# Retention and a gated FFN on one core: the first two pairs of chunks interleaved, their weights in narrower tiles

## The chip, the core and the metric

The kernel runs on one core of a Trainium2 chip. Its engines work side by side, each through its own list of instructions in order: TensorE multiplies matrices (PE in the profile, with PEld for its weight loads), VectorE (DVE) and ScalarE (ACT) read what TensorE left in the PSUM banks and write it to the on-chip memory, GpSimd (POOL) prepares data in that memory, and SyncE (SP) issues the transfers. The metric is the device time of one execution in microseconds, the median of several; lower is better.

## What is computed

```python
scores = (1/8) * q @ k.T                       # 8 batches, 8 heads, 576 positions, 64 dimensions
ret    = scores * gamma[h] ** (i - j)          # for j <= i, else 0
x      = (ret @ v)                             # heads side by side: 4608 rows of 512
out    = (sigmoid(x @ w_gate) * (x @ w_val)) @ w_out     # 512 -> 1536 -> 512
```

The retention is computed in chunks of 128 positions. Within a chunk the masked product of q and k is multiplied with v ("intra"); what comes from earlier chunks is q times a running 64 by 64 state per head, the sum of k times v ("inter"). The powers of gamma are put on q and k when these are cast to bf16.

## The kernel before, in words

x is kept transposed on the chip (`xT`, 512 by 4608) and filled by chunks; the FFN runs over blocks of its columns. The first 768 columns are three *pairs* of chunks (`PAIRS`): pair 0 is positions 0 to 255 of batch 0, pair 1 is positions 256 to 511 of it, pair 2 is the first 256 of batch 1. The rest are 30 *steps* of 128 columns, each loaded, cast, turned by a DMA transposition (`cross`, L294, the tile T) and worked off in a slot between the matmuls of the FFN (`slot`, L543). The schedule is written by hand: each engine gets its instructions in the order in which the program issues them, and waits for semaphores of the others.

The change lies in the start, up to the first FFN block (columns 0 to 511, made from pairs 0 and 1). Its parts, by their functions:

- `load_pair` (L130) and `load_w` (L142) issue transfers of 256 KB on SP. The order now: k and q of both pairs, then v of both, then the first gate and value weights for 256 columns (`load_w(0, 2)`, four tiles of 128 by 2 by 256), then the next 256 columns, then the rest. Each transfer waits until the one eight places before it has landed; the load tiles are 18.
- `cast_pair` makes bf16 of k (with its powers, on POOL, L272), of q (with its powers, on DVE, L272) and of v (POOL, L269); `cast_w` makes bf16 of weights (L246). On POOL: k of both pairs, v of both, the first weights.
- `turn` transposes k or q of two heads pairs on TensorE (`pair_t`, L312) and copies the result with ACT (L322) to kT or qT. It needs a PSUM bank: TR and PV have one buffer each, QK two, the FFN's three, the state's one.
- `pair_qk` multiplies kT and qT (L331, 16 matmuls) and masks the result on DVE (L336, two instructions) to ptp.
- `first_st` adds k times v of one chunk to the state's bank (L362, 8 matmuls), `tile_sv` copies the state to `sbd` on ACT (L371, two instructions).
- `pair_intra` (L429, 8 matmuls) and `pair_inter` (L439, 4 matmuls) make a chunk's x in a bank, `pair_out` (L448) moves it to xT.
- `h_half` (L892) makes 256 columns of one gate or value of the FFN from four matmuls, `gate` (L898) is the sigmoid on ACT, and L895 the product of both on DVE. `h_both` (L816) then goes on with 512 columns at a time, from the third of the 12 pieces of 128 features on.
- `fill` (L183) is matmuls of a blank tile into an unused bank: no part of the result. Before the change there are 40 short ones at the start and four calls with 3, 2, 3 and 2 long ones.

The order now, from the last `fill`: pair 0 and pair 1 are turned and multiplied first (k and q alone), then come the states and values of pair 0, then those of pair 1 with the first two gates of columns 0 to 255 between them, then the remaining halves of the first two features pieces, and `h_both((2, 3))`.

Of the kernel before, what the change touches and what calls it, by code (L numbers as in the profile page):

```python
# [16 lines left out]
def kernel(  # L17
# [19 lines left out]
    nc = tc.nc  # L37
# [87 lines left out]
    def load_pair(A):  # L125

        b, a2 = PAIRS[A]
        for nm, src, g in (("k", k, 0), ("q", q, 0), ("k", k, 1), ("q", q, 1), ("v", v, 0), ("v", v, 1)):
            t = ld_pool.tile([P, M, 2, D], FP32, tag="ld", name=f"{nm}32p_{A}_{g}")
            nc.sync.dma_start(  # L130
                out=t.rearrange("p h r d -> p h (r d)"),
                in_=src[b, g * M:(g + 1) * M, a2 * 2 * P:(a2 + 1) * 2 * P, :].rearrange("h (p r) d -> p h (r d)", r=2))
            parts[nm, "pair", A, g] = t
            yield

    def load_w(f, nf):

        for nm, src in (("g", moe_w_gate), ("v", moe_w_val)):
            for i in range(nf):
                r = NKC // nf  # L140
                t = ld_pool.tile([P, r, nf * P], FP32, tag="ld", name=f"w{nm}32_{f}_{i}")
                nc.sync.dma_start(  # L142
                    out=t, in_=src[i * r * P:(i + 1) * r * P, f * P:(f + nf) * P].rearrange("(c p) f -> p c f", p=P))
                parts[nm, f, i] = t
# [3 lines left out]
        nc.sync.dma_start(out=t, in_=moe_w_out[f * P:(f + 1) * P, :])  # L148
        parts["o", f] = t

    both = [load_pair(A) for A in range(2)]
    for n_pair in (4, 2):
        for one in both:
            for _ in range(n_pair):
                next(one)
    load_w(0, 2)
    load_w(2, 2)
    load_w(4, 4)
    load_w(8, 4)
# [19 lines left out]
    def fill(n, parts=1):  # L179

        for i in range(n * parts):
            k = 4 // parts
            nc.tensor.matmul(idle[-1][:, 0:k, :], lhsT=blank, rhs=blank.unsqueeze(1).to_broadcast([P, k, P]),  # L183
                             start=True, stop=True)
# [58 lines left out]
    def cast_w(nm, f, nf, i, eng):  # L243
        r = NKC // nf
        at = (slice(None), slice(i * r, (i + 1) * r), slice(f * P, (f + nf) * P))
        eng(out=(wg_sb if nm == "g" else wv_sb)[at], in_=parts.pop((nm, f, i)))  # L246
# [12 lines left out]
    def cast_pair(nm, A, g, eng):  # L259

        if (nm, A) not in natural:
            natural[nm, A] = osb_pool.tile([P, 2, H, D], BF16, tag="osb", name=f"{nm}p_{A}")
        if nm != "v" and A == 2:
            o = natural[nm, A].rearrange("p r (m y) d -> p y m r d", y=2)[:, g]
        else:
            o = natural[nm, A][:, :, g * M:(g + 1) * M, :].rearrange("p r h d -> p h r d")
        i = parts.pop((nm, "pair", A, g))
        if nm == "v":
            eng(out=o, in_=i)  # L269
        else:  # L270
            tab = (ktab2 if nm == "k" else qtab2)[:, PAIRS[A][1], g * M:(g + 1) * M, :].unsqueeze(3).to_broadcast([P, M, 2, D])
            eng.tensor_tensor(out=o, in0=i, in1=tab, op=ALU.mult)  # L272
# [51 lines left out]
    def pair_qk(A, g, banks):  # L324
        ps = [psum.tile([P, 2, 2, P], FP32, tag=tag, name=f"qkp_{A}_{g}_{hh}") for hh, (psum, tag) in enumerate(banks)]
        for i in range(2):
            m = 2 * g + i
            for r in range(2):
                for a in range(2):
                    for hh in range(2):  # L330
                        nc.tensor.matmul(ps[hh][half(a), i, r, :], lhsT=turned["kp", A][half(hh), m, r, half(a)],  # L331
                                         rhs=turned["qp", A][half(hh), m, a * P:(a + 1) * P], start=True, stop=True)
        if g == 0:
            probs["p", A] = [att_pool.tile([P, M, 2, P], BF16, tag="T", name=f"ptp_{A}_{hh}", bufs=6) for hh in range(2)]
        for hh in range(2):
            nc.vector.tensor_tensor(out=probs["p", A][hh][:, 2 * g:2 * g + 2], in0=ps[hh],  # L336
                                    in1=trip.unsqueeze(1).to_broadcast([P, 2, 2, P]), op=ALU.mult)
# [18 lines left out]
    def first_st(A, a):  # L356

        if 0 not in st_tiles:
            st_tiles[0] = st_psum.tile([P, M, P], FP32, tag="st", name="st_0")
        for r in range(2):  # L360
            for m in range(M):
                nc.tensor.matmul(st_tiles[0][:, m, :], lhsT=natural["k", A][half(a), r, 2 * m:2 * m + 2, :],  # L362
                                 rhs=natural["v", A][half(a), r, 2 * m:2 * m + 2, :],
                                 start=(A == 0 and a == 0 and r == 0 and m == 0),
                                 stop=(A == 1 and a == 1 and r == 1 and m == M - 1), skip_group_check=True)

    def tile_sv(A, a, engs):
        b, a2 = PAIRS[A]
        sb = sbd[2 * A + a]
        for hh in range(2):  # L370
            engs[hh](out=sb[half(hh), :, half(hh)], in_=st_tiles[b][half(hh), :, half(hh)])  # L371
        state[b, 2 * a2 + a, 1] = sb
# [47 lines left out]
    def pair_intra(A, g, a):  # L420
        s = 2 * A + a
        if s not in pair_ps:
            pair_tile(A, a, [(tr_psum, "tr") if a else (pv_psum, "pv")])
        for i in range(2):
            m = 2 * g + i
            ps, at_m, of = pair_ps[s][m]
            for r in range(2):
                for hh in range(2):
                    nc.tensor.matmul(ps[half(hh), at_m, :], lhsT=natural["v", A][half(a), r, 2 * m + hh, :],  # L429
                                     rhs=probs["p", A][hh][half(a), m, r, :],  # L430
                                     start=(at_m == 0 and r == 0), stop=(at_m == of - 1 and r == 1),
                                     skip_group_check=True)
# [372 lines left out]
    def turn(nm, A, g, pool=ffn_psum, tag="ffn"):  # L805
        pair_t(nm, A, g, pool, tag, on_act)
# [23 lines left out]
    for A in range(2):  # L830
        for g in range(2):
            cast_pair("k", A, g, nc.gpsimd)
    for A in range(2):
        for g in range(2):
            cast_pair("v", A, g, on_pool)
    for i in range(2):
        cast_w("g", 0, 2, i, on_pool)
    for i in range(2):
        cast_w("v", 0, 2, i, on_pool)
    QK = [(qk_psum, "qk"), (qk_psum, "qk")]  # L840
    FF = [(ffn_psum, "ffn"), (ffn_psum, "ffn")]
    TR, PV = (tr_psum, "tr"), (pv_psum, "pv")
    cast_pair("q", 0, 0, nc.vector)
    turn("k", 0, 0, *TR)
    turn("q", 0, 0, *PV)
    fill(3)
    cast_pair("q", 0, 1, nc.vector)
    pair_qk(0, 0, QK)
    turn("k", 0, 1, *TR)
    fill(2)  # L850
    turn("q", 0, 1, *PV)
    fill(3)
    cast_pair("q", 1, 0, nc.vector)
    pair_qk(0, 1, FF)
    cast_pair("q", 1, 1, nc.vector)
    turn("k", 1, 0, *TR)
    turn("q", 1, 0, *PV)
    fill(2)
    turn("k", 1, 1, *TR)
    pair_qk(1, 0, QK)  # L860
    turn("q", 1, 1, *TR)
    first_st(0, 0)
    tile_sv(0, 0, (on_act, on_act))
    for g in range(2):
        pair_intra(0, g, 0)
    pair_qk(1, 1, FF)
    pair_out(0, 0, on_act)
    for g in range(2):
        pair_intra(0, g, 1)
    pair_inter(0, 1)  # L870
    first_st(0, 1)
    tile_sv(0, 1, (on_act, on_act))
    pair_out(0, 1, on_dve)
    for a in range(2):
        pair_tile(1, a, QK[a:a + 1])
    for g in range(2):
        for a in range(2):
            pair_intra(1, g, a)
    pair_inter(1, 0)
    pair_out(1, 0, on_dve)  # L880
    first_st(1, 0)
    tile_sv(1, 0, (on_act, on_act))

    gs = [g_pool.tile([P, 512], BF16, tag="g", name=f"g_0_{fc}") for fc in range(2)]
    for fc in range(2):
        gvs[fc] = gv_pool.tile([P, 512], BF16, tag="gv", name=f"gv_0_{fc}")
# [13 lines left out]
    def h_bank(psum, tag, name, n):  # L900
        return psum.tile([P, n, 256], FP32, tag=tag, name=name)

    g0 = h_bank(ffn_psum, "ffn", "hg_0", 1)[:, 0]
    h_half("g", 0, 0, g0)
    g1 = h_bank(ffn_psum, "ffn", "hg_1", 1)[:, 0]
    h_half("g", 1, 0, g1)
    gate(0, 0, g0)
    pair_inter(1, 1)
    pair_out(1, 1, on_dve, on_act)
    gate(1, 0, g1)  # L910
    first_st(1, 1)
    v0 = h_bank(ffn_psum, "ffn", "hv_0", 2)
    h_half("v", 0, 0, v0[:, 0])
    h_half("g", 0, 1, (g2 := h_bank(qk_psum, "qk", "hg_2", 2))[:, 0])
    h_half("g", 1, 1, g2[:, 1])
    h_half("v", 1, 0, v0[:, 1])
    gate(0, 1, g2[:, 0])
    gate(1, 1, g2[:, 1])
    tile_sv(1, 1, (on_act, on_act))
    for fc in range(2):  # L920
        h_half("v", fc, 1, h_bank(ffn_psum, "ffn", f"hv_{1 + fc}", 1)[:, 0])
    for i in range(2):
        cast_w("g", 2, 2, i, on_pool)
    cast_w("v", 2, 2, 0, on_pool)
    cast_w("v", 2, 2, 1, on_dve)
    later_constants()
    for i in range(4):
        cast_w("g", 4, 4, i, on_pool)
    step(h_both((2, 3)), 4)
# [154 lines left out]
```

## Time and profile before

| | |
|---|---|
| median of 9 runs | 328.91 us (328.54 to 330.19) |
| the profiled execution, its own time | 330.19 us |
| its span | 328.5 us |
| TensorE busy, of the span | 318.0 us, 97% |
| VectorE, ScalarE, GpSimd busy | 150.3, 139.9, 104.3 us |
| granted TensorE clock, all slices | full |
| read from and written to HBM | 37.75 MB, 9.44 MB |

Busy times are unions of the spans of an engine's instructions. A busy TensorE is not one at its peak, since matmuls are pipelined and the ends of their spans are modelled: what counts for a stretch is when its next one can start. The fills count as busy time too: 10 of 128x512 with 2.8 us and 40 of 128x128 with 3.9 us, all in the first 11 us.

### The profile page before, as it was taken

What the parts mean: (1) busy time and instruction counts of PE and PEld (TensorE: products, weight loads), DVE (VectorE), ACT (ScalarE), POOL (GpSimd) and SP (SyncE); (2) the same over time, 40 slices, a digit from 0 to 9 for tenths busy, and PEclk for the clock granted to TensorE, in tenths of its full rate; (3) what the DMA queues carried; (4) which work ended last, traced back from release to release, by engine and by line L of the source; (5) the groups of instructions that cost most, each with busy time, mean ns of one, the idle gap of its engine ahead of it and who ended that gap; (6) DMA issues with size and microseconds to landing.
All of it is one profiled execution on the core that took longest, in us unless ns stands there. A gap on an engine that the chain in (4) does not pass through costs nothing.

```text
span 328.5 us, 8719 instructions
## 1 busy us (share of the span) xinstructions
PE 318.0 (97%) x3584; PEld 170.2 (52%) x3618; DVE 150.3 (46%) x334; ACT 139.9 (43%) x315; POOL 104.3 (32%) x138
## 2 busy tenths in 40 slices
PE   7899999989999999999999999999999999999995
PEld 6664557846646554455444544454445544544443
DVE  5845756666615463445344543334444434404410
ACT  6654545554424344325532453335334533343321
POOL 5784546334554454018300840075003000000000
PEclk9999999999999999999999999999999999999999
DMA  7999999999999999708890799069704910010003
GB/s 214 348 393 380 360 249 187 141 174 209 223 204 197 233 231 220 163 0 215 196 230 4 144 244 254 4 131 234 184 0 108 336 43 0 34 69 31 3 32 96
DMA packets 144793, 55.14 MB, mean 168 GB/s; under 512 B 125168, under 2 KB 136688, under 8 KB 144752
## 3 DMA queue, kind: packets, MB, share of 16 engines
q1 hardware_dynamic: 144608, 54.44, 69.4%
q8 instruction: 28, 0.46, 0.6%
q10 hardware_dynamic: 144, 0.13, 0.1%
q14 instruction: 13, 0.11, 0.1%
HBM read 37.75 MB, written 9.44 MB: 144 GB/s over the span
## 4 chain that ended last, share of the span: by engine, by line
PE 88%; DMA 5%; SPq 2%; issue 1%; POOL 1%; DVE 1%; ACT 0%; ACTq 0%
PE h L712 50%; PE op L779 23%; PE op L963 3%; PE hv L816 3%; PE hg L816 3%; SPq L130 2%; DMA T<-qk 2%; PE val L523 2%; DMA wv<-in_moe_w_val_dram 2%; DMA v32p<-in_v_dram 2%; PE row L497 1%; PE row L505 1%; PE val L539 1%; PE op L768 1%; POOL wg_sb L246 0%
## 5 line engine op out<-in xcount | busy, mean ns | idle before, releaser
L740 DVE TENSOR_TENSOR gv<-g,h 128x512 bf16<-128x512 bf16 (+1 forms) x96 | 62.9, 655 | 103.2 <-PE h L712 100.4
L712 PE MATMUL h<-xT,wg_sb 128*128 128x512 bf16 (+2 forms) x426 | 100.3, 355 | 0.7 <-DVE xT L611 0.3
L712 PE MATMUL h<-xT,wv_sb 128*128 128x512 bf16 (+2 forms) x426 | 100.3, 355 | 0.3
L736 ACT ACTIVATE g<-h 128x512 bf16<-128x512 f32 (+1 forms) x96 | 54.8, 571 | 95.0 <-PE h L712 90.9
L779 PE MATMUL op<-wo_sb,gv 128*128 128x512 bf16 x355 | 80.7, 379 | 2.2 <-issue 2.1
L712 PEld LDWEIGHTS <-wg_sb 128*128 128x128 bf16 x432 | 41.9, 98 | 41.8 <-PE op L779 0.8
L712 PEld LDWEIGHTS <-wv_sb 128*128 128x128 bf16 x432 | 42.0, 98 | 40.4
L779 PEld LDWEIGHTS <-gv 128*128 128x128 bf16 x372 | 35.3, 98 | 40.9
L290 POOL CAST v<-v 128x512 bf16<-128x512 f32 x29 | 17.7, 611 | 95.1 <-PE val L523 83.0
L285 POOL TENSOR_TENSOR qk<-k,ktab 128x512 bf16<-128x512 f32 x30 | 31.5, 1049 | 29.4 <-DMA k<-in_k_dram 22.2
L755 ACT COPY ob<-op 128x512 f32<-128x512 f32 x33 | 19.3, 586 | 35.2 <-PE op L779 32.3
L285 POOL TENSOR_TENSOR qk<-q,qtab 128x512 bf16<-128x512 f32 x28 | 29.2, 1043 | 2.3 <-DMA q<-in_q_dram 2.2
L512 DVE TENSOR_TENSOR pt<-row,tri 128x256 bf16<-128x256 f32 x60 | 21.6, 418 | 14.0 <-PE row L505 12.6
L581 ACT CAST xT<-val 128x256 bf16<-128x256 f32 x46 | 15.0, 380 | 22.7 <-PE val L539 18.0
L624 DVE TENSOR_TENSOR s<-s,row 128x256 f32<-128x256 f32 x39 | 16.3, 417 | 1.3
L473 ACT CAST sb<-s 128x256 bf16<-128x256 f32 x44 | 15.9, 420 | 1.4 <-DVE s L624 1.3
L567 DVE COPY glance<-val 128x1 f32<-128x1 f32 x24 | 2.7, 155 | 23.4 <-PE val L539 22.7
L963 PE MATMUL op<-wo_sb,gv 128*128 128x512 bf16 x45 | 11.4, 379 | 0.3 <-issue 0.2
L497 PE MATMUL row<-T 64*64 64x64 bf16 x480 | 9.8, 197 | 0.3 <-DMA T<-qk 0.3
L523 PEld LDWEIGHTS <-v 64*64 64x64 bf16 x480 | 6.2, 108 | 7.5 <-issue 7.5
L539 PE MATMUL val<-T,sb 64*64 64x64 bf16 x368 | 9.7, 195 | 0.3 <-DVE glance L567 0.3
L336 DVE TENSOR_TENSOR ptp<-qkp,trip 128x512 bf16<-128x512 f32 x12 | 7.6, 685 | 4.4 <-PE qkp L331 4.4
(104 smaller groups left out, 236.9 us busy)
## 6 DMA issues: line engine op xcount, KB each, us to landing
out_dram<-ob SPq DMA_DIRECT2D x31, 256.0 KB, 3.1
k<-in_k_dram SPq DMA_DIRECT2D x26, 256.0 KB, 3.8
q<-in_q_dram SPq DMA_DIRECT2D x26, 256.0 KB, 4.3
v<-in_v_dram SPq DMA_DIRECT2D x26, 256.0 KB, 4.5
wg<-in_moe_w_gate_dram SPq DMA_DIRECT2D x12, 256.0 KB, 5.2
wv<-in_moe_w_val_dram SPq DMA_DIRECT2D x12, 256.0 KB, 5.2
wo<-in_moe_w_out_dram SPq DMA_DIRECT2D x12, 256.0 KB, 5.2
k32p<-in_k_dram SPq DMA_DIRECT2D x6, 256.0 KB, 5.2
```

The source lines that it names most:

```text
L285: eng.tensor_tensor(out=natural_qk[s][:, i].rearrange("p m (y d) -> p y m d", y=2), in0=by_halves(loaded[s][1 - i]), in1=tab, op=ALU.mult)
L290: eng(out=natural["v", s], in_=loaded[s][2])
L473: eng(out=state[key], in_=src)
L512: nc.vector.tensor_tensor(out=probs[s][:, y], in0=row_ps[s][y][:, 0], in1=tri.unsqueeze(1).to_broadcast([P, M, 64]), op=ALU.mult)
L624: nc.vector.tensor_tensor(out=new, in0=running[b], in1=p, op=ALU.add)
L712: nc.tensor.matmul(out, lhsT=w_sb[:, kc, fc * P:(fc + 1) * P], rhs=xT[:, kc, t0 + a:t0 + e], start=(kc == 0), stop=(kc == NKC - 1))
L736: nc.scalar.activation(out=g[:, 0:n], in_=h1[:, 0:n], func=AF.Sigmoid)
L740: nc.vector.tensor_tensor(out=gvs[some[0]][:, a:e], in0=g[:, 0:n], in1=h2[:, 0:n], op=ALU.mult)
L755: (eng or on_act)(out=ob, in_=opp)
L779: nc.tensor.matmul(opp, lhsT=gvs[fc][:, nb * P:(nb + 1) * P], rhs=wo_sb[:, fc, :], start=(fc == 0), stop=(fc == NFC - 1))
L816: nc.tensor.matmul(ps, lhsT=(wg_sb if what == "g" else wv_sb)[:, kc, fc * P:(fc + 1) * P], rhs=xT[:, kc, 0:4 * P], start=(kc == 0), stop=( ...
L963: nc.tensor.matmul(opps[nb], lhsT=gvs[fc][:, nb * P:(nb + 1) * P], rhs=wo_sb[:, fc, :], start=(fc == 0), stop=(fc == NFC - 1))
```

## The change

Transfers: all six of pair 0 are issued first, then one gate and one value tile of 128 columns (four blocks of 128 by 128), then the six of pair 1 and the tiles of the next 128 columns. The bytes are the same. POOL's casts follow that order. On TensorE pair 0 is taken to its end (states, values, x) before pair 1 is turned; its first gate and value, and later those of the second piece of features, stand between the parts of pair 1. Of the fills one call of two long matmuls goes. The two q casts of pair 1 stand behind the last x of pair 0 on DVE, instead of ahead of and behind the masks of pair 0. The last q's turn uses one of the FFN's banks, the values of pair 1 the banks PV and TR instead of QK. The cast of one tile of value weights goes from DVE to ACT, ahead of a copy of the state, and the small constants (`later_constants`) on POOL stand one cast earlier.

```diff
-    both = [load_pair(A) for A in range(2)]
-    for n_pair in (4, 2):
-        for one in both:
-            for _ in range(n_pair):
-                next(one)
-    load_w(0, 2)
+    for A in range(2):
+        for _ in load_pair(A):
+            pass
+        load_w(A, 1)
...
     for A in range(2):
         for g in range(2):
             cast_pair("k", A, g, nc.gpsimd)
-    for A in range(2):
         for g in range(2):
             cast_pair("v", A, g, on_pool)
-    for i in range(2):
-        cast_w("g", 0, 2, i, on_pool)
-    for i in range(2):
-        cast_w("v", 0, 2, i, on_pool)
+        for what in ("g", "v"):
+            cast_w(what, A, 1, 0, on_pool)
...
+    def h_one(what, fc, x):
+        ps = h_bank(ffn_psum, "ffn", f"h{what}_0_{fc}_{x}", 1)[:, 0]
+        h_half(what, fc, x, ps)
+        if what == "g":
+            gate(fc, x, ps)
...
     fill(3)
+    first_st(0, 0)
+    pair_qk(0, 1, FF)
+    tile_sv(0, 0, (on_act, on_act))
+    for a in range(2):
+        pair_intra(0, 0, a)
+    first_st(0, 1)
+    for a in range(2):
+        pair_intra(0, 1, a)
+    pair_out(0, 0, on_act)
+    pair_inter(0, 1)
+    pair_out(0, 1, on_dve)
     cast_pair("q", 1, 0, nc.vector)
-    pair_qk(0, 1, FF)
+    turn("k", 1, 0, *TR)
+    h_one("g", 0, 0)
+    tile_sv(0, 1, (on_act, on_act))
     cast_pair("q", 1, 1, nc.vector)
-    turn("k", 1, 0, *TR)
     turn("q", 1, 0, *PV)
-    fill(2)
+    h_one("v", 0, 0)
     turn("k", 1, 1, *TR)
     pair_qk(1, 0, QK)
-    turn("q", 1, 1, *TR)
-    first_st(0, 0)
-    tile_sv(0, 0, (on_act, on_act))
-    for g in range(2):
-        pair_intra(0, g, 0)
+    turn("q", 1, 1)
     pair_qk(1, 1, FF)
-    pair_out(0, 0, on_act)
-    for g in range(2):
-        pair_intra(0, g, 1)
-    pair_inter(0, 1)
-    first_st(0, 1)
-    tile_sv(0, 1, (on_act, on_act))
-    pair_out(0, 1, on_dve)
-    for a in range(2):
-        pair_tile(1, a, QK[a:a + 1])
-    for g in range(2):
-        for a in range(2):
+    first_st(1, 0)
+    tile_sv(1, 0, (on_act, on_act))
+    h_one("g", 1, 0)
+    for a, bank in enumerate((PV, TR)):
+        pair_tile(1, a, [bank])
+        for g in range(2):
             pair_intra(1, g, a)
     pair_inter(1, 0)
-    pair_out(1, 0, on_dve)
-    first_st(1, 0)
-    tile_sv(1, 0, (on_act, on_act))
...
-    g0 = h_bank(ffn_psum, "ffn", "hg_0", 1)[:, 0]
-    h_half("g", 0, 0, g0)
-    g1 = h_bank(ffn_psum, "ffn", "hg_1", 1)[:, 0]
-    h_half("g", 1, 0, g1)
-    gate(0, 0, g0)
+    pair_out(1, 0, on_act)
     pair_inter(1, 1)
-    pair_out(1, 1, on_dve, on_act)
-    gate(1, 0, g1)
+    pair_out(1, 1, on_dve)
+    h_one("v", 1, 0)
     first_st(1, 1)
-    v0 = h_bank(ffn_psum, "ffn", "hv_0", 2)
-    h_half("v", 0, 0, v0[:, 0])
     h_half("g", 0, 1, (g2 := h_bank(qk_psum, "qk", "hg_2", 2))[:, 0])
     h_half("g", 1, 1, g2[:, 1])
-    h_half("v", 1, 0, v0[:, 1])
     gate(0, 1, g2[:, 0])
     gate(1, 1, g2[:, 1])
+    cast_w("v", 2, 2, 1, on_act)
     tile_sv(1, 1, (on_act, on_act))
     for fc in range(2):
         h_half("v", fc, 1, h_bank(ffn_psum, "ffn", f"hv_{1 + fc}", 1)[:, 0])
     for i in range(2):
         cast_w("g", 2, 2, i, on_pool)
+    later_constants()
     cast_w("v", 2, 2, 0, on_pool)
-    cast_w("v", 2, 2, 1, on_dve)
-    later_constants()
```

`h_half`, `gate` and `h_bank` are the same functions as before, defined further up.

More of the change, by code (lines that the diff above doesn't have):

```diff
@@ L842 @@
     TR, PV = (tr_psum, "tr"), (pv_psum, "pv")
[L843 to L849, printed above, removed]
-    fill(2)
-    turn("q", 0, 1, *PV)
-    fill(3)
-    cast_pair("q", 1, 0, nc.vector)
-    pair_qk(0, 1, FF)
-    cast_pair("q", 1, 1, nc.vector)
-    turn("k", 1, 0, *TR)
[L857 to L860, printed above, removed]
-    turn("q", 1, 1, *TR)
-    first_st(0, 0)
-    tile_sv(0, 0, (on_act, on_act))
-    for g in range(2):
-        pair_intra(0, g, 0)
-    pair_qk(1, 1, FF)
-    pair_out(0, 0, on_act)
-    for g in range(2):
-        pair_intra(0, g, 1)
-    pair_inter(0, 1)
-    first_st(0, 1)
-    tile_sv(0, 1, (on_act, on_act))
-    pair_out(0, 1, on_dve)
-    for a in range(2):
-        pair_tile(1, a, QK[a:a + 1])
-    for g in range(2):
-        for a in range(2):
-            pair_intra(1, g, a)
-    pair_inter(1, 0)
-    pair_out(1, 0, on_dve)
-    first_st(1, 0)
-    tile_sv(1, 0, (on_act, on_act))
     gs = [g_pool.tile([P, 512], BF16, tag="g", name=f"g_0_{fc}") for fc in range(2)]
@@ L901, in h_bank @@
         return psum.tile([P, n, 256], FP32, tag=tag, name=name)
-    g0 = h_bank(ffn_psum, "ffn", "hg_0", 1)[:, 0]
-    h_half("g", 0, 0, g0)
-    g1 = h_bank(ffn_psum, "ffn", "hg_1", 1)[:, 0]
-    h_half("g", 1, 0, g1)
-    gate(0, 0, g0)
+    def h_one(what, fc, x):
[3 more added lines that the diff above has]
+            gate(fc, x, ps)
+    cast_pair("q", 0, 0, nc.vector)
+    turn("k", 0, 0, *TR)
+    turn("q", 0, 0, *PV)
+    fill(3)
+    cast_pair("q", 0, 1, nc.vector)
+    pair_qk(0, 0, QK)
+    turn("k", 0, 1, *TR)
+    fill(2)
+    turn("q", 0, 1, *PV)
+    fill(3)
+    first_st(0, 0)
[9 more added lines that the diff above has]
+    pair_out(0, 1, on_dve)
+    cast_pair("q", 1, 0, nc.vector)
+    turn("k", 1, 0, *TR)
+    h_one("g", 0, 0)
+    tile_sv(0, 1, (on_act, on_act))
+    cast_pair("q", 1, 1, nc.vector)
+    turn("q", 1, 0, *PV)
+    h_one("v", 0, 0)
+    turn("k", 1, 1, *TR)
+    pair_qk(1, 0, QK)
+    turn("q", 1, 1)
+    pair_qk(1, 1, FF)
+    first_st(1, 0)
[4 more added lines that the diff above has]
+        for g in range(2):
+            pair_intra(1, g, a)
+    pair_inter(1, 0)
+    pair_out(1, 0, on_act)
     pair_inter(1, 1)
-    pair_out(1, 1, on_dve, on_act)
-    gate(1, 0, g1)
+    pair_out(1, 1, on_dve)
+    h_one("v", 1, 0)
     first_st(1, 1)
-    v0 = h_bank(ffn_psum, "ffn", "hv_0", 2)
-    h_half("v", 0, 0, v0[:, 0])
     h_half("g", 0, 1, (g2 := h_bank(qk_psum, "qk", "hg_2", 2))[:, 0])
     h_half("g", 1, 1, g2[:, 1])
-    h_half("v", 1, 0, v0[:, 1])
     gate(0, 1, g2[:, 0])
     gate(1, 1, g2[:, 1])
+    cast_w("v", 2, 2, 1, on_act)
     tile_sv(1, 1, (on_act, on_act))
```

## The prediction

> **What bounds the kernel now.** I read the slices of the page first, then the stretches, then TensorE's order of time in the first 22 us, then the chain of waits.
>
> ```profile
> PE   7899999989999999999999999999999999999995
> DMA  7999999999999999708890799069704910010003
> ...
> 0.00:5.40 5.40, 4.20 (x44) 3.91 (x44) 4.02 (x24) 3.77 (x8) 3.10 (x12) 1.00 0.57 156
> 5.40:21.50 16.10, 14.55 (x242) 10.48 (x243) 9.60 (x17) 9.85 (x22) 11.61 (x19) 1.00 1.08 356
> 21.50:63.00 41.50, 41.13 (x439) 24.29 (x443) 26.65 (x51) 21.63 (x47) 20.75 (x29) 1.00 1.01 281
> 63.00:75.00 12.00, 10.93 (x233) 6.60 (x235) 7.78 (x21) 5.45 (x17) 5.24 (x6) 1.00 1.23 177
> 75.00:328.50 253.50, 247.17 (x2633) 124.96 (x2658) 102.30 (x223) 99.18 (x223) 63.60 (x74) 1.00 0.60 137
> ```
>
> The lower five lines are stretches: length, then busy time of PE, PEld, DVE, ACT, POOL, granted clock, DMA share, GB/s. From 21.5 us to 63 TensorE lacks 0.37 us, so whatever the start gains or loses by 21.5 us arrives at 63. From 63 to 75 it lacks 1.07 us: only there can a shift be swallowed. DMA is at its limit in the first 44 us or so.
>
> ```profile
> 11.54 0.42 PE L331 MATMUL qkp<-qT,kT 64*64 64x128 bf16 x16 [0.18 <-ACT qT L322]
> 12.91 0.49 PE L362 MATMUL st<-vp,kp 64*128 64x128 bf16 x6 [0.27 <-POOL vp L269]
> 14.43 0.40 PE L439 MATMUL pvp<-qT,sbd 128*128 128x128 bf16 x4
> 16.22 0.40 PE L439 MATMUL pvp<-qT,sbd 128*128 128x128 bf16 x4 [0.20 <-ACT sbd L371]
> 17.10 1.05 PE L892 MATMUL hg<-xT,wg_sb 128*128 128x256 bf16 x8
> 20.20 1.47 PE L892 MATMUL hv<-xT,wv_sb 128*128 128x256 bf16 x12
> 21.51 0.38 PE L816 MATMUL hg<-xT,wg_sb 128*128 128x512 bf16 x1
> ```
>
> The start as TensorE sees it: its waits on ACT and POOL are short, since one pair's matmuls cover the copies of the other. The mark I follow is the last line: the full-width FFN starts at 21.51 us.
>
> ```profile
> 67.62 6.06 DMA T<-qk
> 73.68 0.04 issue
> 73.73 0.32 PE row L497 x16
> 74.05 0.13 PE row L505 x16
> ```
>
> These are from the chain of waits. A transposed T is issued at 67.62 and lands at 73.68, and TensorE starts on it at 73.73. That T hangs on loads, POOL's casts and SP's queue, none of which waits for these matmuls. So before the change TensorE and the transfers meet at 73.7 with next to no slack: a faster start can bring at most some tenths, a slower one is paid but for what the idle of 63 to 75 absorbs.
>
> **What the Trainium skill says.** "TensorE: Matmul & The Clock Gate", Part 1, table of the two states: after an idle window of about 3.4 us the clock falls to half. Here the granted clock is 1.00 in every stretch, with gaps of at most about half a us; larger ones no run here shows. "GPSIMD Engine Reference", Specifications: GpSimd shares its SBUF interface with VectorE instructions that have two SBUF inputs. The q cast is one, and the trace agrees: it takes 682 to 698 ns as a rule, but 1524 where a k cast runs on POOL (33.97 us). "DMA: Bandwidth & Descriptors", Specifications: at least 512 B are wanted for line rate. The new weight tiles have runs of exactly that. The pairs have it already: 315 GB/s in 5 to 10 us, against 404 in 20 to 25 with longer runs.
>
> **The change part by part.** Durations are from the rows of before. Steps that follow each other on TensorE are counted by what they hold it: 4 transposes 0.22 (result after 0.40), `pair_qk` 0.29 (0.42), `first_st` 0.54, 8 matmuls of `pair_intra` 0.14, `pair_inter` 0.33 (0.40), `h_half` 0.45; ACT: kT 0.59, qT 0.73, state 0.74 (two of 0.37), gate 0.39; DVE: two masks 1.29, x of a chunk 0.68, q cast 0.69; 0.05 for each handover. Put on the order of before, this way of counting gives 21.40 for the mark, against the measured 21.51.
>
> *Transfers.* Places in the queue stay, only their contents change. v of pair 0 takes the places 5 and 6, whose tiles POOL took up at 8.30 and 9.86, or at landing if it was free: with two casts of 0.62 it is ready at about 9.7. k of pair 1 moves from places 5 and 7 to 9 and 11, q to 10 and 12; their data come at about 11.3 to 14.5 instead of 8.2 to 10.5. Four weight tiles in 512 B runs: 0.83 us at 315 GB/s against 0.65 at 404, so at most 0.18 each, 0.7 in all; I take 0.1 each. They aren't on the path: the first gate's weights are cast by 10.7 and used at 13.8. Were the cover gone, the T of 73.68 would be later by 0.4 to 0.7.
>
> *Pair 0.* Up to 9.43 (end of the second qT copy) nothing changes. `first_st` starts with v at 9.74, `pair_qk(0,1)` at 10.28, and its masks run from 10.75 to 12.04. Values of the second half: 12.09, `pair_inter` 12.37 to 12.77, x on DVE 12.82 to 13.50. Before, this `pair_qk` began at 9.48; now it has `first_st` ahead and nothing to fill the wait for its masks.
>
> *Pair 1.* Its first turn needs the bank TR, in which the second chunk of pair 0 lies until DVE has read it: 13.55 instead of 9.84. Then ACT is the chain: kT 14.00 to 14.59, first gate to 14.98, state to 15.72, qT to 16.45. `pair_qk(1,0)` starts at 16.50 after a gap of 1.37 on TensorE; the last turn's result comes at 17.19, its copy runs from 17.24 to 17.97, and `pair_qk(1,1)` starts at 18.02 after a gap of 1.0. Masks 18.49 to 19.78. Values with the last masks from 19.83, three groups of 0.14, two `pair_inter` of 0.33: 20.91, the last result at 20.98. x on DVE 21.03 to 21.71, beneath a value piece and `first_st` on TensorE, which end at 21.90. Then the four halves over columns 256 to 511, 4 x 0.45: the mark at 23.70. That is 2.3 later than the same count for before.
>
> *What costs nothing.* The fill removed held TensorE 0.44 us, which becomes waiting. A q cast that meets POOL's k cast at 13.8 may take 1.5 instead of 0.7, but the gap of 1.37 takes that up, as ACT is late there anyway. Without that cover it is 0.8. The weight cast on ACT (0.62 instead of 0.69 on DVE) ends at 24.0 and is needed at 25.4. `later_constants` (0.7 on POOL) moves one cast ahead; the gate weights of the next four pieces are then ready at about 23.6 and used at 27. Behind the delayed q casts on DVE wait only masks that are later anyway. The buffers they free, in places 10 and 12, are asked for by transfers issued at 20.2 and after. Clock: gaps of 1.4 and 1.0 are well short of the window; I take 0, at most half speed through one window, 1.7.
>
> *From the mark to the end.* 2.25 late at 63. T at 73.68 does not move with TensorE (or by 0.4), so the wait of 0.3 before L497 goes. A further wait of 0.35 at 72.20 for x on DVE: two copies of the state there stretched over 1.83 us beside POOL's casts; TensorE and DVE come later than these casts now, so I let 0.3 go. What is late next is TensorE itself. Sum: 2.25 - 0.3 - 0.3 = 1.65, from 0.8 (all idle of 63 to 75 is swallowed, and 0.4 less at the start) to 2.7 (nothing swallowed, 0.4 more). The span goes from 328.5 to about 330.15. The profiled execution, 330.19 with 1.7 around its span, is the slowest of the nine, so I put the difference on the median: 328.91 + 1.65 = 330.6.
>
> **The rivals.**
> *The start is no longer than before* (not slower). The new order replaces filling by gates and values. If the handovers of pair 1 hide beneath these, the mark stays at 21.5 or comes earlier; for it speak 2.8 us of fills and the 1.5 us of idle in 5.4 to 21.5. Against it: pair 1's chain of turn, copy, product, mask, value, copy can't start before its data, which are 3 us later, and its TR bank. It decides if that chain is shorter by 2.2 us than I count. Even then T at 73.68 holds: -0.3 to +0.2, 328.8.
> *The transfers become the bound.* The start is on time, but the narrow tiles push T back by 0.4: 329.3. For it the meeting at 73.7, against it that TensorE should be late itself.
> *The clock falls* in the gaps near 16 and 18 us: 330.6 + 1.7 = 332.3. For it, fewer fills; against, gaps below half a window.
>
> **How the numbers follow.** Forecast 0.75, its own range 329.7 to 331.6; start not longer 0.13 (0.06 faster, 0.07 the same); transfers 0.05; clock 0.07. About 0.2% (0.66 us) is what a measurement tells from no change. The forecast's low end and part of the third case's lie near that bound: 0.02 of them go to the same. Faster 0.06, the same 0.09, slower 0.85. The range from 329.2 to 332.2 leaves out nearly all of the first rival and half of the clock's.
>
> **What would show it.** The mark L816 at 23.7 (21.0 to 21.8 is the first rival); TensorE gaps of about 1.4 and 1.0 us on qT at 16.5 and 18.0; the first turn of pair 1 at 13.5 on DVE's x; no wait for T near 74 to 76; a granted clock below 1.00 would be the third rival; T of that slot landing by 74.1, later is the second. The forecast is wrong if the mark is before 22.7, or if over 1.3 us of the shift vanish by 80 us.

## The result, and the profile after

The changed kernel takes 331.63 us, the median of 10 executions (330.61 to 332.35), against 328.97 us of 32 of the kernel before (328.54 to 330.19). The ratio is 1.0079, with an interval from 1.0069 to 1.0088: slower, by about 2.6 us.

The two profiled executions alone would have told something else. That of before took 330.19 us, the slowest of its 32, with a span of 328.5; that of after took 330.99, below its median, with a span of 329.3. Their spans differ by 0.8 us, less than a third of what the medians do. How that comes is half of this study. (On TensorE the two pairs were interleaved before and are taken one after the other now; what is interleaved now are pair 1 and the first gates and values of the FFN.)

The slices of the page of after, TensorE's row:

```profile
PE   7789999999999999999999999999999999999995
```

The stretches of after, those of the prediction (length, then busy time of PE, PEld, DVE, ACT and POOL with the number of instructions, granted clock, DMA share, GB/s):

```profile
5.40:21.50 16.10, 12.33 (x228) 8.85 (x225) 9.72 (x15) 8.96 (x18) 11.18 (x19) 1.00 1.07 337
21.50:63.00 41.50, 41.13 (x440) 24.45 (x442) 24.23 (x46) 21.68 (x46) 24.11 (x31) 1.00 1.04 301
63.00:75.00 12.00, 11.62 (x245) 7.59 (x245) 7.39 (x24) 6.94 (x23) 5.30 (x6) 1.00 0.92 176
```

From 5.40 to 21.50 us TensorE lacks 3.8 us, where it lacked 1.55; from 21.50 to 63 it is as full as it was. On the page it shows in the second and third slice, 7 and 8 where 8 and 9 stood. TensorE's order of time shows its places (start, duration, what; in brackets the idle time just before and what ended it):

```profile
12.21 0.40 PE L437 MATMUL pvp<-qT,sbd 128*128 128x128 bf16 x4
13.39 0.38 PE L310 MATMUL kTp<-ident,kp 128*128 128x128 bf16 x4 [0.78 <-DVE xT L446]
14.68 0.40 PE L310 MATMUL qTp<-ident,qp 128*128 128x128 bf16 x4 [0.47 <-DVE qp L270]
16.11 0.42 PE L329 MATMUL qkp<-qT,kT 64*64 64x128 bf16 x16 [0.38 <-ACT qT L320]
17.68 0.42 PE L329 MATMUL qkp<-qT,kT 64*64 64x128 bf16 x16 [0.82 <-ACT qT L320]
...
23.58 1.67 PE L814 MATMUL hg<-xT,wg_sb 128*128 128x512 bf16 x7
25.09 1.89 PE L814 MATMUL hv<-xT,wv_sb 128*128 128x512 bf16 x8
```

The mark, the start of the full-width FFN (L814 now, L816 before), needs care. Its first group has 8 matmuls and 7 are recorded, so the first is missing. The values after it start at 25.09; 8 matmuls at 0.216 us earlier is 23.36, and that is the mark of after. The chain of waits of after shows what ACT does between the first turn of pair 1 and the first product that uses it:

```profile
13.81 0.59 ACT kT L320
14.39 0.28 ACT g L852
14.68 0.24 ACT sbd L369
14.92 0.01 issue
14.94 0.37 ACT sbd L369
15.30 0.03 issue
15.33 0.74 ACT qT L320
16.07 0.04 issue
16.11 0.42 PE qkp L329 x16
```

Four pieces of work stand in a row on one engine: the kT copy, the gate, the state (in two copies) and the qT copy, and TensorE starts 0.04 us after the last.

### The profile page after: what moved, and what is told of

It reads as the page before. It is cut to its first block, busy times and chain, and to the rows that moved or that the text cites. A ratio compares the mean times of both kernels' runs of the same rounds, so it can differ in the third digit from the quotient of the medians.

```text
span 329.3 us, 8713 instructions
## 1 busy us (share of the span) xinstructions
PE 317.4 (96%) x3582; PEld 170.6 (52%) x3616; DVE 148.6 (45%) x332; ACT 140.4 (43%) x316; POOL 104.6 (32%) x138
## 3 DMA queue, kind: packets, MB, share of 16 engines
q1 hardware_dynamic: 145632, 54.44, 67.2%
## 4 chain that ended last, share of the span: by engine, by line
PE 93%; DMA 1%; issue 1%; ACT 1%; DVE 1%; POOL 0%; SPq 0%; ACTq 0%
PE h L710 50%; PE op L777 24%; PE op L956 3%; PE hv L814 3%; PE hg L814 3%; PE val L521 2%; DMA k32p<-in_k_dram 1%; PE row L495 1%; PE row L503 1%; PE val L537 1%; PE op L766 1%; PE qkp L329 1%; PE st L360 1%; PE hg L846 0%; ACT qT L320 0%
## 5 line engine op out<-in xcount | busy, mean ns | idle before, releaser
L565 DVE COPY glance<-val 128x1 f32<-128x1 f32 x24 | 2.8, 155 | 23.3 <-PE val L537 22.6
L821 DVE TENSOR_TENSOR gv<-g,hv 128x512 bf16<-128x512 bf16 x10 | 6.8, 687 | 7.0 <-PE hv L814 7.0
```

## The experiments

What had to be told apart: the theory that the start is 2.3 us longer by this chain and that all of it arrives at the end, the clock adding the rest; that the transfers with their narrow weight tiles take part; that it is the clock alone; and, within the start, whether the late data of pair 1 or the order of the work counts. Each kernel was timed beside the kernel before on the same chip (329.06 to 329.09 us there); ratios are against that one. Lines are numbered for each kernel by itself.

**The kernel before once more** (no edit), since its first profile was its slowest execution.

> The kernel before, unchanged, for a second profile. Theory A (the profile on record was of a slow execution: 330.19 us, the highest of 32, with 1.07 us of TensorE idle between 63 and 75 us): the new profile has a span near 327.3 us, less than 0.5 us of idle between 63 and 75 us and no wait for T at the fifth slot, so there is nothing in which a later start could be absorbed. Theory B (that idle is in every execution): again about 1.0 us of idle there, and the changed kernel's loss of 2.66 us must come from somewhere after 75 us. Time 329.0 in both.

It took 329.1 us (14 executions, ratio 1.0004, 0.9991 to 1.0017), its profiled one 328.71 us, the lowest of the 14 and 0.4 below their median, with a span of 327.0. One of the 14 had a clock of 0.990 and took 331.75; it is the only one of 79 executions of this kernel with their clocks on record that fell below 0.998. The stretches of this run, TensorE only:

```profile
5.40:21.50 16.10, 15.31 (x249) 1.00 1.10 365
...
63.00:75.00 12.00, 11.79 (x239) 1.00 0.91 147
```

From 63 to 75 us TensorE lacks 0.21 us here, against 1.07 in the profile that the prediction read. The order of time on TensorE has the mark at 21.05, not 21.51:

```profile
21.05 1.89 PE L816 MATMUL hg<-xT,wg_sb 128*128 128x512 bf16 x7
```

And the T that landed at 73.68 there was issued much earlier here. The SP queue's order of time, and the chain of waits near its use, both of this run:

```profile
62.38 1.96 SPq L294 DMA_TRANSPOSE T<-qk  x1
```

```profile
72.04 0.25 PE val L523 x16
72.29 0.13 PE val L539 x16
72.42 0.13 PE row L497 x16
```

Issued at 62.38 with 4.8 us to landing, this T is there at 67.2, 5 us before TensorE takes it at 72.4; in the first profile it came 0.05 us before its use. The same place in the chain of waits of after:

```profile
74.35 0.25 PE val L521 x16
74.59 0.13 PE val L537 x16
74.72 0.13 PE row L495 x16
```

That is 2.3 us later than in this run, the same as the mark (23.36 against 21.05) and the same as the span (329.3 against 327.0). Between these two executions nothing of the shift is lost on the way.

**Blank matmuls in the four gaps** of after: 11 of 128x512, no part of the result.

```diff
+    fill(3)
     turn("k", 1, 0, *TR)
     h_one("g", 0, 0)
+    idle_bank()
+    fill(2)
...
+    fill(2)
     pair_qk(1, 0, QK)
     turn("q", 1, 1)
+    fill(4)
     pair_qk(1, 1, FF)
```

> The changed kernel with 11 blank matmuls put into its four waits on TensorE (12.4, 14.1, 15.6 and 16.7 us), which compute nothing of the result. The changed kernel showed a mean granted clock of 0.993 to 0.995 in 6 of 11 executions. Theory A (the gaps let the clock fall, and that costs about 1 us where it happens): clock 1.000 in every execution, median 331.2 us, spread below 0.8 us. Theory B (the clock falls for another reason, or the lower clock costs nothing): clock and median as in the changed kernel, 331.6. The start of the full-width FFN stays at 23.4 us in both, since the fills fit into the waits; if they don't, it goes to 23.8.

331.06 us (330.78 to 331.47, five executions), ratio 1.0054 (1.0042 to 1.0066), below after's interval. The clock was 0.998 or more in all five. Of after's 11 executions (the profiled one among them) five have that too, with a median of 331.21; the other six have 0.993 to 0.995 and 331.52 to 332.35. The two groups' means are 331.07 and 331.98. So the executions with the lower clock are about 0.9 us longer; they are somewhat over half, and the median is 0.4 above that of the others (331.63 against 331.21). The rest, 2.2 us, stands with a full clock, and 2.0 with the blank matmuls: the missing fill explains at most the smaller part. That the blank matmuls held the clock is likely, not shown: five executions are few, and the version with another bank below held it in five too, without any.

**The fills only before the two products of pair 1** (the last two calls above and `idle_bank`).

> The changed kernel with blank matmuls in the last two of its four waits alone (before the two products of pair 1, at 15.6 and 16.7 us). Theory A (the clock falls because of the half-empty stretch from 15.6 to 17.7 us): clock 0.998 or more in every execution, median 331.1. Theory B (the waits at 12.4 and 14.1 us count as much, or the first ones do): clock of 0.993 to 0.995 in some executions, median 331.4 or more.

330.92 us (330.39 to 331.94, six executions), ratio 1.0063 (1.0047 to 1.0078). Two of the six still had a clock of 0.995, with 331.75 and 331.94. So these fills alone do not rule the fall out. Whether the two earlier gaps bring it, six executions can't tell, and the trace that was kept is of one with a full clock.

**One half of the change each.** First the transfers and POOL's casts of after, with before's order of work:

```diff
-    both = [load_pair(A) for A in range(2)]
...
+    for A in range(2):
+        for _ in load_pair(A):
+            pass
+        load_w(A, 1)
```

> The kernel before with the changed order of transfers and GpSimd casts alone (narrow tiles, v and first weights of pair 0 ahead of pair 1), TensorE in the old order. Theory A (the new order of data only serves a TensorE that takes pair 0 to its end first): the first turn of pair 1 waits for its k until 12.4 us, full-width FFN at about 24.9 us, time about 332.4. Theory B (the order of data is not what costs, the order of work is): full-width FFN by 21.7, time 329.0.

336.17 us, scattered from 332.24 to 336.91, with clocks of 0.994 down to 0.978; ratio 1.0171 (1.0124 to 1.0218). The longest of TensorE's waits up to 24 us (sum, times, longest), and two of its stretches, in the profiled execution (336.82, clock 0.978, mark at 28.73):

```profile
PE kTp L310 <- POOL kp L270: 2.2, 1, 2.2
```

```profile
13.00:26.70 13.70, 13.60 (x165) 0.50 1.07 383
26.70:30.00 3.30, 3.25 (x25) 1.00 1.02 346
```

The old order asks for pair 1's k before it is there, once, for 2.2 us, and then runs at half clock for 13.7 us though TensorE is busy all along. The lowest execution, 332.24, loses some 3.2 us. Its clock was 0.994; if that takes the 0.9 us that it took in after, about 2.3 are left (an estimate), close to the wait.

Then after's order of work with before's transfers and casts (the rest of the change without the lines above):

> The changed kernel with the old order of transfers and GpSimd casts (k and q of both pairs first, weights of 256 columns), TensorE, VectorE and ScalarE in the new order. Theory A (new order of work and new order of data need each other): the first product of k and v waits from 9.2 to about 12.8 us for v, full-width FFN at about 26.4, time about 334.3, and more where the clock falls in that wait. Theory B (the new order of work is not what costs, the late data of pair 1 are): full-width FFN at or before 22, time near 329.5.

335.47 to 336.00 us in three executions (a fourth, 340.67, on a lower clock still), ratio 1.0204 (1.0185 to 1.0222). Waits, and TensorE's order of time at the mark:

```profile
PE st L362 <- POOL vp L269: 2.9, 2, 2.5
```

```profile
27.42 1.89 PE L816 MATMUL hg<-xT,wg_sb 128*128 128x512 bf16 x8
```

Now pair 0's v comes too late for an order that wants it first: 2.9 us of waits, and then 6.9 us at a clock of 0.51. The two halves belong together: alone they cost 3.2 us or more and 6.7 us, together 2.66, the clock included each time. How much of the 6.7 is the waits and how much the clock was not taken apart.

**The narrow weight tiles alone**, at the place of the old ones in before:

```diff
-    load_w(0, 2)
+    load_w(0, 1)
+    load_w(1, 1)
```

> The kernel before with the first weights in tiles of 128 columns alone (runs of 512 B instead of 1 KB), at their old places in the queue. Theory A (0.1 to 0.18 us a tile, hidden): weights of the next pieces land 0.4 to 0.7 later, full-width FFN as before at 21.0 to 21.2, time 329.0. Theory B (the transfers bound the kernel before): time 329.4 to 329.7.

329.25 us (13 executions), ratio 1.0009 (1.0001 to 1.0017): 0.3 us, at most 0.6. The narrow tiles are not what costs 2.6. The profiled execution (329.16, span 327.4) has the mark at 21.51, as the first profile of before had, and yet lacks only 0.17 us from 63 to 75.

**The state's copies moved on ACT**, from behind the first gate to ahead of the first turn of pair 1:

```diff
     first_st(0, 1)
+    tile_sv(0, 1, (on_act, on_act))
...
     h_one("g", 0, 0)
-    tile_sv(0, 1, (on_act, on_act))
```

> The changed kernel with the copy of pair 0's second state (0.74 us on ScalarE) moved out of the chain kT, gate, state, qT of pair 1 to where it can run while ScalarE waits (11.5 us). Theory A (ScalarE's row of copies between 13.8 and 17.6 us sets when the products of pair 1 start): they start 0.5 to 0.75 earlier, full-width FFN at 22.6 to 22.9 instead of 23.36, time lower by 0.5 to 0.75. Theory B (VectorE's q casts, 1.97 us beside GpSimd, set it): full-width FFN at 23.2 to 23.4, time as in the changed kernel.

331.14 us (330.33 to 331.68, six executions, three of them at a clock of 0.995), ratio 1.0056 (1.0042 to 1.0069). In TensorE's order of time:

```profile
13.75 0.38 PE L310 MATMUL kTp<-ident,kp 128*128 128x128 bf16 x4 [0.78 <-DVE xT L446]
...
15.98 0.42 PE L329 MATMUL qkp<-qT,kT 64*64 64x128 bf16 x16 [0.16 <-ACT qT L320]
```

From the first turn to the product it is 2.23 us instead of 2.72: the two copies cost about 0.5 where they stood. The turn itself was 0.36 later in this execution, in which v of pair 0 was cast 0.37 later, so the mark moved by little (23.23). ACT's row is shown as a cause for half a us between turn and product. At the end it is not shown: the mark was expected between 22.6 and 22.9, and the three executions with a full clock (330.33, 330.86, 331.44) lie on both sides of the 331.21 that after takes with a full clock.

**The first turn of pair 1 in another bank**, ahead of pair 0's last copy:

```diff
+    turn("k", 1, 0, *QK[0])
     pair_out(0, 1, on_dve)
     cast_pair("q", 1, 0, nc.vector)
-    turn("k", 1, 0, *TR)
```

> The changed kernel with the first turn of pair 1 in a bank of QK instead of TR, ahead of pair 0's last x. Theory A (the wait of 0.78 us for that x is on the path): the turn starts at 12.5 instead of 13.4, the gap moves to the first gate, which needs the same x; the copy kT leaves ScalarE's row of copies, the product of pair 1 starts 0.4 earlier, full-width FFN at 23.0, time 0.4 lower. Theory B (VectorE's q casts set that product): full-width FFN at 23.3 to 23.4, time as in the changed kernel, 331.6.

330.71 us (330.64 to 330.88, five executions, clock 0.998 or more), ratio 1.0049 (1.0037 to 1.0061).

```profile
12.38 0.39 PE L310 MATMUL kTp<-ident,kp 128*128 128x128 bf16 x4
13.34 0.61 PE L846 MATMUL hg<-xT,wg_sb 128*128 128x256 bf16 x4 [0.56 <-DVE xT L446]
14.36 0.40 PE L310 MATMUL qTp<-ident,qp 128*128 128x128 bf16 x4 [0.42 <-DVE qp L270]
```

The turn comes 1.0 us earlier, but the product only 0.3 (15.80) and the mark 0.3 (23.06): DVE's x and q cast are the next to be late. The bank is worth 0.3 us of the mark. The clock held in these five, though the waits of 0.56, 0.42, 0.38 and 0.82 us up to the second product stayed open.

**Other orders of the same work.** One with after's data (the values by halves as their masks come, the pair's first q cast amid pair 0, other banks, the value pieces late), one likewise with before's data. The first, cut:

```diff
+    pair_tile(0, 0, [PV])
+    pair_intra(0, 0, 0)
+    cast_pair("q", 1, 0, nc.vector)
...
+    turn("k", 1, 0, *PV)
+    turn("q", 1, 0, *FF[0])
-    cast_pair("q", 1, 0, nc.vector)
-    turn("k", 1, 0, *TR)
-    h_one("g", 0, 0)
-    tile_sv(0, 1, (on_act, on_act))
...
```

> The data of the changed kernel (its transfers and casts), with another order of the same work and other banks on the three engines: the q casts of pair 1 ahead of pair 0's last x, its first turn not in the bank that waits for that x, pair 0's second state copied before it, the last q turned before the last product's masks. Theory A (the chain of handovers makes the loss, of which about 1.2 us is its order and banks and about 1.1 us the later data of pair 1): full-width FFN at 22.1 to 22.4, no wait above 0.8 us on TensorE after 9 us, clock 1.0 throughout, time 330.1 to 330.4. Theory B (the later data make all of it): full-width FFN at 23 or later, time 331 or more.

330.35 us (330.05 to 331.0, five executions, clock 0.999 or more), ratio 1.0041 (1.0029 to 1.0054); the mark in TensorE's order of time:

```profile
22.69 1.67 PE L814 MATMUL hg<-xT,wg_sb 128*128 128x512 bf16 x7
```

> A try at a version faster than both: the data order of the kernel before, with the same work in an order that the durations of the profile suggest. By these the full-width FFN starts 0.3 earlier than before, at 20.75, and the time falls to 328.7. If the waits of VectorE's q casts beside GpSimd are longer than counted it is the same as before, 329.0.

329.03 us (328.34 to 331.91, 13 executions; the two slowest at a clock of 0.990), ratio 1.0004 (0.9984 to 1.0023), mark at 20.83. So with after's data the order and the banks are worth some 0.7 us of mark; 1.3 us over before remain in the best order I found (1.6 of mark). The trace of that order has waits on the later data themselves: POOL stood 1.68 us for v of pair 1 and DVE twice 0.7 for its q, and TensorE then waited 0.66 us for that v and 0.27 for a q. That the data make all of the 1.3 is argued, not shown: a version with pair 1's k and q ahead of the weights was not tried.

**That order with before's data, with four blank matmuls more**: two each before the last turn of k and of q.

```diff
+    idle.append(tr_psum.tile([P, 4, P], FP32, tag="tr", name="idle_1"))
+    fill(2)
     turn("k", 1, 1, *FF[0])
...
+    fill(2)
     turn("q", 1, 1, *FF[0])
```

> The try at a faster version again, with four blank matmuls in its two waits on TensorE (before the turns of pair 1's second k and q), since its clock fell to 0.99 in 2 of 13 executions, which took 331.4 and 331.9, and the best five took 328.3 to 328.5. Theory A (the clock): no execution above 329.6, median 328.4 to 328.9. Theory B (the fills delay the turns): full-width FFN at 21.1, median 329.0 or more.

328.54 us (328.21 to 329.05, 15 executions, clock 0.999 or more in all), ratio 0.9987 (0.9979 to 0.9994). It is ahead of both kernels; over before by 0.13%, less than the 0.2% that the prediction took as its bound, though the interval leaves out 1. The profiled execution is the slowest of the 15 and has its mark at 21.35, later than before's 21.05, so this trace does not show where the gain is. The clock fell in two of 13 executions without these fills and in none of 15 with them, which is no proof that they hold it.

## Why the prediction was right, and where it was not

*The start: right, link by link.* The first turn of pair 1 was to be at 13.55 and was at 13.39, held by DVE's x as said; the two products were to be at 16.50 and 18.02 and were at 16.11 and 17.68, both behind ACT's qT; from the second product to the mark it was 5.68 us in the sum and 5.68 in the trace. The mark was 23.70 in the sum and 23.36 in the trace; of these 0.34 us, 0.2 were there from the first state of pair 0 on, at 9.54 in the chain of waits instead of 9.74. Against the second profile of before it moved by 2.31 us, with 2.3 predicted.

*One gap was two.* The gap of 1.37 before the first product became 0.47 and 0.38, with the first gap ended by a q cast on DVE. Two of these casts took 1.97 us beside POOL's k cast, where 0.7 each was the rule and 1.5 the fear. That "the gap of 1.37 takes that up" was nearly right: with the state's copies moved, DVE still held the qT turn for 0.19 us and ACT the product for 0.16 (from the trace of that run), and with the other bank the cast was next at 0.42. So the casts were about as late as ACT, and a repair of ACT alone brought only 0.5 between turn and product.

*Transfers: right in direction.* Taken at 0.1 us a tile and hidden; the narrow tiles alone cost 0.3 us, from nearly nothing to 0.6. The second rival had T as the end of all; no wait for T stood near 74 us in after.

*The step that failed: "Sum: 2.25 - 0.3 - 0.3 = 1.65".* The two terms taken off were idle time of 63 to 75 us: the wait for T, and a wait of 0.35 for x. Both were real in the profile that was read, and they are in none of the others. In the twelve profiles taken later, of the kernel before, of after and of the variants, TensorE lacks 0.17 to 0.38 us in that stretch, and it waits for no T there. From the mark to the end of the span it is 305.9 to 306.4 us in all twelve, whether the mark stands at 20.83 or at 28.73; in the first profile it is 307.0. So a later start arrives at the end whole, within the half us by which these differ; in after and in the second profile of before both are 305.9. The terms measure 0.0 and 0.0, and the prediction of the median should have carried the whole 2.3 (which it counted, and then put down as 2.25).

The statement that TensorE and the transfers "meet at 73.7 with next to no slack" was of one execution. The reason given for a T that stays, that "none of which waits for these matmuls", is contradicted by the chain of the very profile that was read, just ahead of that T:

```profile
64.07 1.87 PE h L712 x16
...
66.40 0.17 ACT xT L597
66.57 0.01 SPq L118
...
67.49 0.02 SPq L294
```

Here SP's load (L118), which stands ahead of the transposition, waits for ACT's copy of an x that TensorE made (L597). So the issue of T is not free of TensorE. In after this T was issued at 63.65, in the second profile of before at 62.38; how much of that is the later start and how much chance, two executions don't tell.

The own time of 330.19 at the upper end of "328.54 to 330.19" stood ready as a warning; the sum was instead made in that execution and the difference put on the median. Of its 1.5 us over the span of the second profile, 1.3 lie in two places: 0.46 in the mark and 0.86 from 63 to 75.

*The second term: "Clock: gaps of 1.4 and 1.0 are well short of the window; I take 0".* It fell in six of 11 executions, which are 0.9 us longer, and makes 0.4 in the median. With the 2.31 of the mark that is 2.7, against 2.66 measured. The rival of the clock had the right event, with 1.7 for each time too high and a chance of 0.07 that looks low beside six of 11. That the gaps near 16 and 18 us bring it is not shown.

*Direction and range* held: 331.63 lies within 329.2 to 332.2. It lies just beyond the forecast's own 329.7 to 331.6, whose upper end was set by "nothing swallowed", with 0.4 more at the start. Nothing was swallowed; the start was not longer than counted, and the clock, put at 0, made up the rest. Both missed terms, 0.6 and 0.4, point the same way, and the forecast of 330.6 is what the fastest execution of after took (330.61).

## What to carry to other kernels

Before idle time deep in a kernel is credited with swallowing a shift, look where the profiled execution stands among the timed ones; if it is at the edge, the idle time may be its own. A second profile tells, and so does the time from a mark to the end, compared over several profiles. Where two chains of matrix product and copy run beside each other, taking one to its end first can bring the copies of the other one behind each other on one engine, as here on ACT: count that engine's list between the first matrix product and the last, and count what the bank still holds. Reordering the loads and reordering the work were one change here: each half cost more than the whole.

## What the hardware showed that was not expected

The granted clock fell without a long idle window. The Trainium skill, "TensorE: Matmul & The Clock Gate", Part 1, table of the two states, names an idle window of about 3.4 us as what brings half speed. The waits here are shorter. In the kernel with after's data and before's order, a single recorded wait of 2.2 us ended at 12.09, and from 13.0 on 13.7 us followed at a clock of 0.50 with TensorE busy; in the kernel with after's order and before's data, waits of 2.5 and 0.5 us were followed by this (stretches of TensorE):

```profile
8.00:13.90 5.90, 2.73 (x54) 1.00 1.13 354
13.90:20.80 6.90, 5.97 (x65) 0.51 1.08 388
20.80:24.00 3.20, 2.37 (x62) 1.00 1.05 406
```

In after the clock fell in six executions of 11. The gaps of 0.78, 0.47, 0.38 and 0.82 us within 6 us are of an execution in which it did not fall; none in which it fell was kept. With blank matmuls in these gaps it fell in none of five, in the version with the other bank, with similar gaps left open, in none of five either, and in the unchanged kernel in one of 79. So a long fall followed waits shorter than that window, in two traces; whether short gaps add up, and how many of them it takes, is not settled by these runs.

The instants at which transfers are issued and land vary more than the time of the kernel does: the same T was issued at 62.38 in one execution and landed at 67.2, and in another at 67.62 and 73.68, while the two spans differ by 1.5 us. The mark of the unchanged kernel was at 21.05 and at 21.51.
